# A GEGLU feed-forward kernel: TensorE transposes one block of x instead of two, and the early loads change queues

## The chip, the core and the metric

The kernel runs on one NeuronCore of a Trainium2 chip. Its engines work side by side, each through its own list of instructions, and meet at semaphores: TensorE (PE: matmuls, with weight loads as PEld), VectorE (DVE), ScalarE (ACT), GpSimd (POOL) and SyncE (SP). SP and ACT also issue DMAs, each into a queue of its own (q1 is SP's and q10 ACT's in the profile); the transfers of both run on the same 16 DMA engines. The metric is the device time of one execution in microseconds: 271.39 us, the median of four runs (271.34 to 272.06).

## The reference

x is 1024 x 1024 (32 x 32 tokens of 1024), the gate and up weights are 1024 x 3584, the down weight is 3584 x 1024, all bf16.

```python
def _gelu(x):
    return jax.nn.gelu(x, approximate=True)
...
    B, S, D, F = 32, 32, 1024, 3584
...
def reference(x, w_gate, w_up, w_down):
    return (_gelu(x @ w_gate) * (x @ w_up)) @ w_down
```

## The kernel before

**Tiling.** The 1024 of D are DK = 8 blocks of 128 (k), the 3584 of F are FM = 28 blocks of 128 (m). A matmul holds a 128 x 128 block of a weight (its stationary operand) and streams 512 tokens of x with D on the partitions, so x is needed transposed: `xT[0]` (`x0`) is the first 512 tokens as 8 blocks of 128 x 512, `xT[1]` (`x1`) the other 512. Gate and up results of four m at a time fill the eight PSUM banks, bank 2m + j with j = 0 for gate and 1 for up.

**Stages.** First come the blocks m = 0 to 9 for the first 512 tokens, in ordinary bf16 matmuls. Their weights sit in two buffers `quad[0]` (m = 0 to 3) and `quad[1]` (m = 4 to 7), each 2 (gate, up) x 8 (k) x 512 columns. Then 14 pairs of m go through a seven-product scheme on sums and differences of operands (lines 236 to 484), in fp32r, and last the product with the down weight in the same manner (487 to 616).

**The order of work.** `_Program` collects the instructions. TensorE's run in the order in which they are added; those of every other engine are sorted by a planned time `at` and, at the same `at`, by the order of adding (line 88). Each instruction waits for the last writer of what it reads and for the readers of what it overwrites; nothing else orders the engines. One DMA has one semaphore, so that one load of two k-blocks tells of both at once. All the instructions stand under line 117 in the profile, where they are emitted.

**The first 12 us.** All of this has `at` = 0, so the order in the code is the order in the queues:

- Lines 200 to 201: TensorE warms up with six matmuls of 512 columns and two of 128 on constants.
- Lines 203 to 205: NX = 2 blocks (k = 0 and 1) of x, as it lies in memory, go into `xn`, a view of the last block of `hT`. SP brings tokens 0 to 255 and ACT tokens 256 to 511, 128 KB each.
- Lines 210 to 213: `load_quad(eng, q, j, k0, k1)` loads columns of quad q, gate or up j, k-blocks k0 to k1. SP issues the four gate blocks (q = 0 and 1, k = 0 and 1), ACT the four up blocks, 128 KB each.
- Lines 214 to 215: SP issues DMA transposes of x blocks 2, 3, 4, 5 and of 6 and 7 together, from memory into `xT[0]`.
- Lines 216 to 218: ACT issues k = 2 and 3 of quad 1, gate and up in turn, and then loads its table for GELU (line 219).
- Lines 220 to 225: TensorE transposes the eight 128 x 128 pieces of `xn`, two to a PSUM bank, and VectorE copies four times two of them into `xT[0]`.
- Lines 262 to 267: quad 0 with k = 0 and 1: for each k four gate matmuls, then four up matmuls. After k = 1 the sums are copied to `kept`, by ACT for even m and by VectorE for odd m; quad 0 goes on with k = 2 to 7 much later.
- Lines 268 to 270: ACT issues k = 4 to 7 of quad 1 (`at` 9 and 10).
- Lines 273 to 287: quad 1 with all k, eight matmuls per k up to k = 5, then k = 6 and 7 one m after another. When the first matmul with k = 2 has run (`begin_late`), SP may issue k = 2 to 7 of quad 0. At `at` = 12 come the transposes of `xT[1]` (line 317).

Of the kernel before, what the change touches and what calls it, by code (L numbers as in the profile page):

```python
# [6 lines left out]
P = 128  # L7
BF16 = mybir.dt.bfloat16
# [115 lines left out]
def bass_standalone__geglu_ffn__sampling_kernel(  # L124
# [11 lines left out]
    DK, FM = D // P, F // P  # L136
# [3 lines left out]
    x_r = xf.rearrange("(tc p) d -> p tc d", p=P)  # L140
# [3 lines left out]
    pr = _Program()  # L144

    with ExitStack() as es:
        def sb(name, shape, dtype):
            return es.enter_context(nc.sbuf_tensor(name, shape, dtype))

        hT = sb("hT", [P, FM, N], BF16)  # L150
# [5 lines left out]
        ident = sb("ident", [P, P], BF16)  # L156
        warm = sb("warm", [P, 2], FP32)
        p1 = sb("p1", [P, 512], FP32)
        ps = es.enter_context(nc.psum_tensor("ps", [P, 8, 512], FP32))
        const0 = nc.const_aps.tensor(0.0, [P, 1], FP32)  # L160

        xT = [arena[:, a:a + 4096].rearrange("p (k n) -> p k n", n=512) for a in (16384, 0)]
        quad = [arena[:, a:a + 8192].rearrange("p (j k c) -> p j k c", j=2, k=DK) for a in (20480, 8192)]
        def duo(a): return arena[:, a:a + 4096].rearrange("p (j k c) -> p j k c", j=2, k=DK)
        wd = [[arena[:, a:a + 7168].rearrange("p (k n) -> p k n", n=512) for a in row] for row in ((0, 7168), (14336, 21504))]
        xn = hT[:, FM - 1, :].rearrange("p (t c) -> p t c", c=2 * P)
        Sf = S[:, :, :].bitcast(FP32)
        Tf = T[:, :, :, :, :].bitcast(FP32)
        T2r = T[:, :, :, :, :].rearrange("p u j k c -> p (u j k c)").rearrange("p (s n) -> p s n", n=512)
# [9 lines left out]
        def mm(bank, lhsT, rhs, start, stop, held=False, add=False):  # L179
            return pr.add("pe", held_matmul if held else "matmul", ps[:, bank, 0:rhs.shape[-1]], lhsT, rhs,  # L180
                          start=start, stop=stop, skip_group_check=add)
# [4 lines left out]
        def act(out, a, f, at):  # L186
            return pr.add("act", "activation", out, a, f, at=at)

        def dma(eng, out, a, at, name, after=()):
            return pr.add(eng, "dma_start", out, a, at=at, dma=name, after=after)  # L190
# [6 lines left out]
        pr.add("pool", "memset", ident[:, :], 0.0)  # L197
        pr.add("pool", "affine_select", ident[:, :], ident[:, :], [[-1, P]], ALU.not_equal, 1.0,
               base=0, channel_multiplier=1)
        for n in [512] * 6 + [P] * 2:  # L200
            mm(3, one[:, 0:P], one[:, 0:n], True, True)

        NX = 2
        for i, eng in enumerate(("sp", "act")):
            dma(eng, xn[:, 2 * i:2 * i + 2, :], x_r[:, 2 * i:2 * i + 2, 0:NX * P], 0, f"xn{i}")

        def load_quad(eng, q, j, k0, k1, at=0, after=()):
            dma(eng, quad[q][:, j, k0:k1, :], w_r[j][:, k0:k1, 4 * q * P:4 * (q + 1) * P], at, f"w{q}_{j}_{k0}", after)

        for q in range(2):  # L210
            for k in range(NX):
                load_quad("sp", q, 0, k, k + 1)
                load_quad("act", q, 1, k, k + 1)
        for k0, k1 in ((2, 3), (3, 4), (4, 5), (5, 6), (6, 8)):
            pr.add("sp", "dma_start_transpose", xT[0][:, k0:k1, :], xf[0:512, k0 * P:k1 * P], dma=f"x{k0}_0")
        for k in range(2, 4):
            for j in range(2):
                load_quad("act", 1, j, k, k + 1)
        act(warm[:, 0:1], const0, GELU, 0)
        for k in range(NX):  # L220
            for i, b in enumerate((6, 7) if k == 0 else (4, 5)):
                half = ps[:, b, 0:P].bitcast(BF16)
                for t in range(2):
                    pr.add("pe", "transpose", half[:, t * P:(t + 1) * P], xn[:, 2 * i + t, k * P:(k + 1) * P], ident[:, :])
                pr.add("dve", "tensor_copy", xT[0][:, k, i * 256:(i + 1) * 256], half)

# [3 lines left out]
        def piece(a): return a.rearrange("p t n -> p (t n)").bitcast(FP32).rearrange("p (j n) -> p j n", j=2)  # L232
        kept = [piece(hT[:, m:m + 2, :]) for m in (14, 16, 18, 20, 22, 24, 26, 10, 12)] + [piece(o11[:, :, :])]
# [10 lines left out]
        bank = lambda b: ps[:, b, :]  # L244

        def copy(eng, out, a, at):
            if eng == "act":
                act(out, a, COPY, at)
            else:
                pr.add("dve", "tensor_copy", out, a, at=at)  # L250
# [3 lines left out]
        def raw(m, j, k, b, start):  # L254
            return mm(b, quad[m // 4][:, j, k, m % 4 * P:(m % 4 + 1) * P], x0[:, k, :], start, k in (NX - 1, 3, DK - 1), add=not start and k >= NX)
# [6 lines left out]
        for k in range(NX):  # L262
            for j in range(2):
                for m in range(4):
                    raw(m, j, k, 2 * m + j, k == 0)
                    if k == NX - 1:
                        copy(("act", "dve")[m % 2], kept[m][:, j, :], bank(2 * m + j), 6.5 + 0.9 * j + 0.1 * m)
        for i, k in enumerate((4, 6)):
            for j in range(2):
                load_quad("act", 1, j, k, k + 2, 9 + i)  # L270
# [376 lines left out]
```

## Time and profile before

| what | value |
|---|---|
| median of four runs | 271.39 us |
| the profiled execution, its own time | 271.35 us |
| its span, first to last instruction | 269.8 us |
| granted TensorE clock, mean | 1.000 |
| ACT's eight weight loads, issues | 1.25 to 5.37 us |
| ACT's table load | 5.40 to 6.68 us |
| SP's x load, issue, and time from issue to landing | 0.74 us, 2.6 us |
| ACT's x load, issue, and time from issue to landing | 0.73 us, 2.8 us |
| quad 0, k = 0: gate and up, issue to landing | 2.7 and 3.0 us |
| quad 1, k = 1: gate and up, issue to landing | 4.9 and 5.1 us |
| matmul of 512 columns on real data, spacing from 4.59 us on | 0.216 us |

A row of the profile's timeline gives start and duration in us, the engine (with q: its issuing side), the line, the operation, output and inputs by name, how many, and in brackets the engine's idle time before it with what ended it. The chain of waits is followed back from the last instruction: at each step to what released it, or to the instruction before it on its engine. For matmuls the durations overlap, so that spacing counts. In a table of stretches the columns are the stretch, busy time and count for PE, PEld, DVE, ACT and POOL, the granted clock, the mean busy share of the DMA engines (it can pass 1 where packets overlap) and GB/s. A DMA row gives out<-in, the queue, the operation, how many, KB each where it is known, and us from issue to landing.

### The profile page before, as it was taken

How to read it: one execution, taken by the hardware profiler on the slowest of the kernel's cores; microseconds unless marked ns; L12 is line 12 of the kernel's file. 1: busy time of each engine (PE TensorE's matmuls, PEld its weight loads, DVE VectorE, ACT ScalarE, POOL GpSimd, SP SyncE). 2: the span in 40 equal slices, each digit the busy share in tenths (PEclk: the TensorE clock that was granted, in tenths of full speed). 3: DMA queues.
4: the chain of work that ended last, by engine and by line, in shares of the span. 5: the costliest groups of instructions: out<-in, count | busy, mean ns of one | idle time of the engine just before them, and what ended most of it. 6: DMA issues, size and time to landing. Idle time of an engine off the chain costs nothing.

```text
span 269.8 us, 3324 instructions
## 1 busy us (share of the span) xinstructions
PE 266.4 (99%) x1197; PEld 192.1 (71%) x1206; DVE 208.2 (77%) x246; ACT 136.0 (50%) x221; POOL 37.2 (14%) x23
## 2 busy tenths in 40 slices
PE   8999999999999999999999999999999999999997
PEld 3444448888888888888777676664458888888884
DVE  1348998898889889988764839289976999999921
ACT  1349876656766676667455564521220305057452
POOL 1000003203311331134345060000000000000000
PEclk9999999999999999999999999999999999999999
DMA  7999750130591002962900080293010000002102
GB/s 219 239 334 238 215 159 4 57 98 0 153 291 25 0 1 79 291 215 87 227 0 0 0 266 9 91 343 114 0 39 19 4 0 0 0 0 80 58 21 97
DMA packets 45024, 27.47 MB, mean 102 GB/s; under 512 B 8656, under 2 KB 45008, under 8 KB 45008
## 3 DMA queue, kind: packets, MB, share of 16 engines
q1 hardware_dynamic: 42496, 25.04, 33.2%
q10 hardware_dynamic: 2512, 2.23, 3.0%
q8 instruction: 9, 0.15, 0.2%
q14 instruction: 7, 0.06, 0.1%
HBM read 23.33 MB, written 2.10 MB: 94 GB/s over the span
## 4 chain that ended last, share of the span: by engine, by line
PE 99%; DVE 0%; issue 0%
PE ps L117 99%; DVE arena L117 0%; DVE o L117 0%
## 5 line engine op out<-in xcount | busy, mean ns | idle before, releaser
L117 PE MATMUL ps<-S,T 128*128 128x512 f32 x560 | 129.2, 391 | 0.0
L117 PEld LDWEIGHTS ps<-S,T 128*128 128x128 f32 x560 | 105.1, 188 | 22.4
L117 ACT ACTIVATE tmp<-ps 128x512 f32<-128x512 f32 x64 | 38.0, 596 | 51.7 <-PE ps L117 51.5
L117 POOL TENSOR_TENSOR T<-arena 128x1024 fp32r<-128x1024 bf16 x17 | 36.5, 2155 | 123.4 <-PE ps L117 81.7
L117 PE MATMUL ps<-T,S 128*128 128x512 f32 x224 | 51.3, 390 | 0.0
L117 DVE TENSOR_TENSOR T<-arena,T 128x1024 fp32r<-128x1024 bf16 x42 | 50.9, 1218 | 0.2
L117 PEld LDWEIGHTS ps<-T,S 128*128 128x128 f32 x224 | 42.0, 188 | 8.8
L117 ACT ACTIVATE ps<-ps 128x512 f32<-128x512 f32 x44 | 25.6, 583 | 37.0 <-PE ps L117 37.0
L117 DVE TENSOR_TENSOR hT<-tmp,ps 128x512 bf16<-128x512 f32 x56 | 37.0, 684 | 8.7 <-PE ps L117 6.7
L117 PE MATMUL ps<-arena 128*128 128x512 bf16 x186 | 41.6, 379 | 0.6 <-DVE arena L117 0.3
L117 DVE TENSOR_TENSOR tmp<-ps,tmp 128x512 f32<-128x512 f32 x28 | 19.4, 692 | 23.5 <-PE ps L117 23.5
L117 PEld LDWEIGHTS ps<-arena 128*128 128x128 bf16 x192 | 18.2, 98 | 23.1 <-issue 1.4
L117 DVE TENSOR_TENSOR T<-arena 128x1024 fp32r<-128x1024 bf16 x25 | 30.0, 1219 | 4.4 <-PE ps L117 4.3
L117 DVE TENSOR_TENSOR ps<-ps,tmp 128x512 f32<-128x512 f32 x32 | 22.3, 696 | 3.0 <-PE ps L117 3.0
L117 PE MATMUL ps<-arena,hT 128*128 128x512 bf16 (+2 forms) x124 | 24.3, 355 | 0.1
L117 PEld LDWEIGHTS ps<-arena,hT 128*128 128x128 bf16 x126 | 11.7, 98 | 12.7 <-issue 0.5
L117 ACT ACTIVATE tmp<-tmp 128x512 f32<-128x512 f32 x28 | 17.5, 630 | 2.4 <-DVE tmp L117 2.1
L117 ACT ACTIVATE ps<-hT 128x512 f32<-128x512 f32 x22 | 13.0, 598 | 7.6 <-DVE hT L117 7.6
L117 DVE TENSOR_TENSOR S<-hT 128x1024 fp32r<-128x1024 bf16 x14 | 16.6, 1218 | 0.0
L117 ACT ACTIVATE T<-arena 128x1024 fp32r<-128x1024 bf16 x14 | 14.8, 1059 | 0.0
L117 PE MATMUL ps<-S 128*128 128x512 f32 x56 | 12.9, 389 | 0.0
L117 ACT ACTIVATE hT<-ps 128x512 f32<-128x512 f32 x18 | 9.4, 600 | 5.9 <-PE ps L117 5.9
(33 smaller groups left out, 93.8 us busy)
## 6 DMA issues: line engine op xcount, KB each, us to landing
arena<-in_w_down_dram SPq DMA_DIRECT2D x4, 1792.0 KB, 9.6
arena<-in_w_gate_dram SPq DMA_DIRECT2D x10, 512.0 KB, 4.9
arena<-in_w_up_dram SPq DMA_DIRECT2D x10, 512.0 KB, 6.0
out_dram<-arena SPq DMA_DIRECT2D x12, 128.0 KB, 1.7
arena<-in_w_up_dram ACTq DMA_DIRECT2D x6, 128.0 KB, 5.0
arena<-in_w_gate_dram SPq DMA_DIRECT2D x3, 256.0 KB, 5.4
arena<-in_w_up_dram SPq DMA_DIRECT2D x3, 256.0 KB, 5.8
arena<-in_w_gate_dram SPq DMA_DIRECT2D x4, 128.0 KB, 4.6
```

Source lines behind the costliest of these rows:

```text
L117: ins = name(eng, *args, **kw) if callable(name) else getattr(eng, name)(*args, **kw)
```

## The change

TensorE transposes only block 0 of x. `xn` shrinks to 128 columns, so SP and ACT each load 64 KB of x. Block 1 becomes the first of SP's DMA transposes. SP issues only one weight load before them, the gate of quad 0 with k = 0; ACT issues the up of quad 0 with k = 0, then gate and up of quad 0 with k = 1, of quad 1 with k = 0 and 1 in one load of 256 KB each, and of quad 1 with k = 2 and 3 in the same way. The warm-up becomes five matmuls of 512 columns and one of 128. The copies of quad 0 to `kept` change places between ACT and VectorE. The order of the matmuls on real data stays.

```diff
-        xn = hT[:, FM - 1, :].rearrange("p (t c) -> p t c", c=2 * P)
+        xn = hT[:, FM - 1, 0:4 * P].rearrange("p (t c) -> p t c", c=P)
...
-        for n in [512] * 6 + [P] * 2:
+        for n in [512] * 5 + [P]:
             mm(3, one[:, 0:P], one[:, 0:n], True, True)
 
         NX = 2
         for i, eng in enumerate(("sp", "act")):
-            dma(eng, xn[:, 2 * i:2 * i + 2, :], x_r[:, 2 * i:2 * i + 2, 0:NX * P], 0, f"xn{i}")
+            dma(eng, xn[:, 2 * i:2 * i + 2, :], x_r[:, 2 * i:2 * i + 2, 0:P], 0, f"xn{i}")
...
-        for q in range(2):
-            for k in range(NX):
-                load_quad("sp", q, 0, k, k + 1)
-                load_quad("act", q, 1, k, k + 1)
-        for k0, k1 in ((2, 3), (3, 4), (4, 5), (5, 6), (6, 8)):
+        load_quad("sp", 0, 0, 0, 1)
+        load_quad("act", 0, 1, 0, 1)
+        for q, k0, k1 in ((0, 1, 2), (1, 0, 2), (1, 2, 4)):
+            for j in range(2):
+                load_quad("act", q, j, k0, k1)
+        for k0, k1 in ((1, 2), (2, 3), (3, 4), (4, 5), (5, 6), (6, 8)):
             pr.add("sp", "dma_start_transpose", xT[0][:, k0:k1, :], xf[0:512, k0 * P:k1 * P], dma=f"x{k0}_0")
-        for k in range(2, 4):
-            for j in range(2):
-                load_quad("act", 1, j, k, k + 1)
         act(warm[:, 0:1], const0, GELU, 0)
-        for k in range(NX):
-            for i, b in enumerate((6, 7) if k == 0 else (4, 5)):
-                half = ps[:, b, 0:P].bitcast(BF16)
-                for t in range(2):
-                    pr.add("pe", "transpose", half[:, t * P:(t + 1) * P], xn[:, 2 * i + t, k * P:(k + 1) * P], ident[:, :])
-                pr.add("dve", "tensor_copy", xT[0][:, k, i * 256:(i + 1) * 256], half)
+        for i in range(2):
+            half = ps[:, 6 + i, 0:P].bitcast(BF16)
+            for t in range(2):
+                pr.add("pe", "transpose", half[:, t * P:(t + 1) * P], xn[:, 2 * i + t, :], ident[:, :])
+            pr.add("dve", "tensor_copy", xT[0][:, 0, i * 256:(i + 1) * 256], half)
...
-                        copy(("act", "dve")[m % 2], kept[m][:, j, :], bank(2 * m + j), 6.5 + 0.9 * j + 0.1 * m)
+                        copy(("dve", "act")[m % 2], kept[m][:, j, :], bank(2 * m + j), 6.5 + 0.9 * j + 0.1 * m)
```

## The prediction

> **What bounds the kernel now.** I read the page first, for the engine shares and the chain of waits; then the chain in order of time, to see where TensorE ever stands still; then the timeline of the first 12 us with the DMA issues one by one; then stretches of that time with the DMA rate in each.
>
> ```profile
> span 269.8 us, 3324 instructions
> PE 266.4 (99%) x1197; PEld 192.1 (71%) x1206; DVE 208.2 (77%) x246; ACT 136.0 (50%) x221; POOL 37.2 (14%) x23
> ...
> PE 99%; DVE 0%; issue 0%
> ```
>
> ```profile
> 0.78 3.16 PE ps L117 x10
> 3.93 0.02 issue
> 3.96 0.50 DVE arena L117 x2
> 4.46 0.14 issue
> 4.59 7.28 PE ps L117 x33
> ...
> 191.12 76.87 PE ps L117 x355
> 268.02 0.29 DVE o L117
> ```
>
> The reader is to see that from 4.59 us to 268.02 us the end is set by TensorE alone (the "issue" pieces of 0.05 to 0.07 us in between are lost records). So the change can do two things only: move the 4.59, and open a hole behind it. Whatever lies off TensorE costs nothing until a matmul waits for it. The profiled execution took 271.35 us, 1.55 us more than its span; the median of the runs is 271.39. The sum is made against 271.35.
>
> The order of early matmuls is fixed: quad 0 with k = 0 (4 gate, 4 up), with k = 1 (8 more), then quad 1 with k = 0, 1, 2 and so on, eight per k. One takes 0.216 us (33 in 7.28, less one lost record). From 4.59 that gives the time at which each operand is first wanted now: k = 1 of quad 0 at 4.59 + 8 x 0.216 = 6.32; quad 1 gate 8.05, its up 8.91; quad 1 with k = 2 at 11.50, its up 12.37. The rows show how near the present loads come:
>
> ```profile
> 1.26 1.87 SPq L117 DMA_DIRECT2D arena<-in_w_gate_dram  x4
> 3.17 7.53 SPq L117 DMA_TRANSPOSE arena<-in_x_dram  x5
> 6.29 2.93 PEld L117 LDWEIGHTS ps<-arena 128*128 128x128 bf16 x15 [0.31 <-DMA arena<-in_w_gate_dram]
> ```
>
> The weight load at 6.29 waited for the second gate block; it landed 4.5 us after its issue at 1.75, at 6.25, just in time for 6.32. There is no slack at that point. Quad 1's blocks land at 6.95 to 7.85, some 1.0 to 2.2 us early, and x block 2 at 9.23, 2.3 us early.
>
> **The change part by part.**
>
> *Start.* The warm-up loses one matmul of 512 (0.43, the spacing of its weight loads at 2.44, 2.86, 3.29) and one of 128 (0.11): it ends at 0.78 + 5 x 0.427 + 0.107 = 3.02 instead of 3.50. Four of eight transposes and two of four copies (0.28 each) go. The transposes also wait for x, which lands now at 3.36 (SP) and 3.55 (ACT). The new loads have as many packets at half the size. No row has this load; one bound is that it lands as now, the other is that 512 packets on 16 engines each save the 9 ns between the trace's 512-byte packets (27 ns) and its 256-byte ones (18 ns), 0.29 us. From the third transpose (3.72) to the second copy (4.16) are 0.45 us, the copy takes 0.28, the matmul follows 0.15 later. With x there at 3.07 and 3.26 the first matmul starts at about 4.15, with x as now at 4.45. I take 4.25, a gain of 0.34 us. The copies removed were hidden behind matmuls.
>
> *x block 1.* SP has x at 0.74, gate k = 0 at 1.26, and then the transpose at 1.75 instead of three more gates. The other five transposes follow at 1.25 to 1.31 us each (2.3 for the last): 3.0, 4.3, 5.6, 6.9, 8.2, each about 0.17 earlier than now. Two rows bound the landing:
>
> ```profile
> arena<-in_x_dram SPq DMA_TRANSPOSE x1, 6.1
> ```
>
> ```profile
> arena<-in_x_dram SPq DMA_TRANSPOSE x1, 3.5
> ```
>
> The first is the present first transpose (issue 3.17), the second one of two blocks at 21.62 with no weight loads beside it. So block 1 lands between 5.25 and 7.85; wanted at 4.25 + 1.73 = 5.98. The 6.1 contains a wait behind four gates in SP's queue, of which only one is left in front now: the first transpose landed 1.6 us after the last of these gates (7.61). First gate at 3.7 + 1.6 = 5.3; with the 2.1 that lay between the first two transposes, 5.8. I take 5.6: in time, with little to spare.
>
> *Quad 0, k = 1.* Gate and up are now ACT's third and fourth issue (1.80, 2.28); the nearest rows landed at 6.45 and 7.14, with one packet in the lot held 1.4 us. Less x stands before them now. I take 5.2 and 5.8 against wants of 5.98 and 6.84.
>
> *Quad 1.* All of its early weights go to ACT's queue as four loads of two k-blocks, the gate of k = 0 and 1 at 2.76. ACT has eight issues instead of nine, at 0.45 to 0.68 each, so its table load (1.28) starts at about 5.0 instead of 5.40 and it is free for copies at 6.5; the first bank is due at 6.35 and now goes to VectorE, which is idle then. The swap of copies costs nothing; with that cover gone bank 0 is still free by 7.1, wanted at 7.7. What does matter: a load of two blocks tells of its landing once, so the block of k = 1, wanted at 9.77 and 10.63 before, has to be there at 8.05 and 8.91 with that of k = 0. And SP, which carried half of these weights, now carries only transposes from 3 us on. Until now they began to move after 6.1. The stretches show what they do to the rate (the last two numbers are the DMA share and GB/s):
>
> ```profile
> 5.25:6.25 1.00, 1.00 (x6) 0.38 (x4) 0.00 (x0) 0.85 (x1) 0.00 (x0) 1.00 1.08 366
> 6.25:7.25 1.00, 1.00 (x7) 0.49 (x6) 0.30 (x1) 0.99 (x3) 0.00 (x0) 1.00 1.97 251
> 7.25:7.75 0.50, 0.50 (x4) 0.23 (x3) 0.50 (x2) 0.50 (x2) 0.00 (x0) 1.00 0.16 32
> 7.75:8.50 0.75, 0.75 (x6) 0.32 (x4) 0.75 (x2) 0.75 (x3) 0.00 (x0) 1.00 0.93 296
> 8.50:9.50 1.00, 1.00 (x6) 0.38 (x5) 0.93 (x2) 0.35 (x1) 0.00 (x0) 1.00 1.33 244
> 9.50:10.50 1.00, 1.00 (x7) 0.53 (x6) 0.00 (x0) 0.00 (x0) 0.00 (x0) 1.00 1.54 165
> 10.50:11.25 0.75, 0.75 (x5) 0.31 (x4) 0.00 (x0) 0.00 (x0) 0.00 (x0) 1.00 1.04 212
> ```
>
> Weights alone move at 366 GB/s; from 6.25 to 11.25, with transposes among them, the mean is 211, and at 7.25 to 7.75 both queues stand. By the time the up load of quad 1 (k = 0, 1) has landed, the new order has moved x (131 kB), quad 0's and quad 1's blocks (1049 kB) and three transposes (393 kB): 1573 kB. By 3.25 us some 310 kB of it are through (352 now, 131 fewer of x, 88 more in the 0.29 us saved). 1263 kB at 211 take 5.99 us: 9.24, and 0.4 from last packet to landing, as for the first x load: 9.64. At 366 it would be 7.1, at 165 it would be 11.3. By a third way, the bytes alone, the present kernel had landed as much at about 9.2. I take 211, since transposes now run through the whole stretch.
>
> *Sum.* The up matmuls of quad 1 start at 9.64 instead of 8.91: +0.73, in which the early start is already used up. Behind that the later wants move too, by the same 0.73; the up load of k = 2, 3 has to move some 786 kB more (524 and two transposes) at 211, so it lands at 13.4 against 12.37 + 0.73 = 13.1: 0.3 more at worst, in the range. 271.35 + 0.73 = 272.1.
>
> The Trainium skill, Advanced Engine Details and Errata, section X-Bar Transpose (TRN2), says that transposing transfers are as fast as ordinary ones. The stretches above speak against it: 366 without, 211 with them. By the rule the up load would land at 7.1 and the time would be 271.0.
>
> **Rivals.** *All in time* (not slower): transposes give way to ACT's 1024-byte packets, or fewer than three are through by 9 us. Then only the start counts, 4.25 for 4.59: 271.0, at best 270.9. For it: at 7.75 to 8.50 nearly all that moved was ACT's, at 296. Against it: the two stretches after. It decides if the up load lands before 8.57.
>
> *A draw by bytes*: the queues reach the 9.2 of the present order: +0.3, 271.65.
>
> *x block 1 is late*: its landing is the 7.85 of the present first transpose, and TensorE stands from 5.98 on: 7.85 - 6.32 = +1.5, 272.9. For it: a packet of a weight block was held 1.4 us at 3.87, and the first transpose's packets stood until 7.85, about when SP's last gate landed. A transpose that waits for the slowest DMA engine has no slack in the new order. It decides from a landing after 6.32.
>
> *The clock stays low*: the warm-up matmuls run 0.43 us apart, those from 4.59 on 0.216, so the clock rose in between. With 0.5 us less warm-up and a gap before the first matmul it may rise one such period later: the 3.2 us from 0.78 to about 4.0 once more, to 7.2. (7.2 - 4.25)/2 = 1.5 lost, 0.34 gained: +1.1, 272.5. Against it: the gap grows by some 0.3 us only.
>
> The Trainium skill, TensorE: Matmul & The Clock Gate, section Part 4: PE-mode transpose, says that transposes do not count as work for the clock. The trace can't show that alone; if so, the busy part before 4.0 falls from 2.7 to 2.2 us, which favours this rival.
>
> **How the numbers follow.** Forecast (late weights, 271.9 to 272.6) 0.36; late x 0.12; low clock 0.10; a draw 0.20; all in time 0.22. Slower by over 0.2% (0.54 us, about what a measurement of this kernel can tell from no change) are the first three: 0.58. Within it: the draw and most of the last, 0.36. Faster: what is left of the last, 0.06, since even the best start gives 0.48. The likeliest time is 272.1. The range goes from 271.0 to 273.0: below, all in time; above, late x or the 165 GB/s in part. The forecast's own range is 271.9 to 272.6.
>
> **What would show it.** Start right: the first matmul of 512 on real data at 4.15 to 4.45, four transposes. Late weights: a weight-load wait on w_up (ACT's queue) of 0.5 to 1.2 us near 8.5, transposes moving from 3.3 on, rates near 211 GB/s. Late x: the wait stands at 6 and names in_x. Low clock: matmuls 0.43 apart after 4.25. It is wrong if TensorE has no hole before 13 us, or a hole after it.

## The result, and the profile after

| | before | changed |
|---|---|---|
| median | 271.66 us (74 runs) | 272.21 us (53 runs) |
| lowest, highest | 271.31, 272.48 | 271.51, 273.9 |
| ratio of the times | | 1.0018, 95% interval 1.0011 to 1.0024 |
| the profiled execution, its span | 271.35, 269.8 | 271.91, 270.6 |

The changed kernel is slower by 0.55 us, and with so many runs that is clear of chance. It lies on the 0.2% bound of the prediction: the ratio of 1.0018 is just inside, the difference of the medians, 0.55 for 0.54 us, just outside. With 74 runs the median of before stands 0.27 us above the 271.39 of its first four.

The page of the changed kernel's profile, its span and engine shares:

```profile
span 270.6 us, 3304 instructions
PE 267.0 (99%) x1191; PEld 191.9 (71%) x1200; DVE 207.7 (77%) x244; ACT 136.2 (50%) x221; POOL 37.2 (14%) x23
```

The chain of waits in order of time (start, us, what), changed kernel:

```profile
0.78 2.63 PE ps L117 x8
3.40 0.02 issue
3.42 0.52 DVE arena L117 x2
3.94 0.14 issue
4.08 9.87 PE ps L117 x39
...
191.93 76.87 PE ps L117 x355
268.80 0.02 issue
268.82 0.29 DVE o L117
```

The first real matmul starts at 4.08 instead of 4.59, so 0.51 us are won there; and yet the last piece starts 0.8 us later. From 4.08 us on there is no hole on the chain: TensorE stands still for no load. The loss shows only in the spacing of the matmuls. The timeline of weight loads, changed kernel:

```profile
4.05 0.14 PEld L117 LDWEIGHTS ps<-arena 128*128 128x128 bf16 x2 [0.71 <-DMA arena<-in_w_gate_dram]
4.46 0.15 PEld L117 LDWEIGHTS ps<-arena 128*128 128x128 bf16 x1 [0.28 <-issue]
4.88 0.15 PEld L117 LDWEIGHTS ps<-arena 128*128 128x128 bf16 x1 [0.28 <-issue]
5.31 0.15 PEld L117 LDWEIGHTS ps<-arena 128*128 128x128 bf16 x1 [0.28 <-issue]
5.74 0.15 PEld L117 LDWEIGHTS ps<-arena 128*128 128x128 bf16 x1 [0.28 <-issue]
6.17 0.15 PEld L117 LDWEIGHTS ps<-arena 128*128 128x128 bf16 x1 [0.28 <-issue]
6.59 2.76 PEld L117 LDWEIGHTS ps<-arena 128*128 128x128 bf16 x13 [0.28 <-issue]
9.52 0.26 PEld L117 LDWEIGHTS ps<-arena 128*128 128x128 bf16 x2 [0.17 <-DMA arena<-in_w_up_dram]
```

The weight loads are 0.43 us apart until 6.59, as in the warm-up, and then 0.22: the matmuls ran at half speed to about 6.7. The first up matmul of quad 1, the 21st on real data, started at 9.68; at 0.216 a matmul it would have been 4.08 + 20 x 0.216 = 8.40. So the low clock cost 1.28 us in this execution; less the 0.51 won at the start that is 0.77, nearly the whole difference of the spans (0.8). The last row shows the other thing. Quad 1's up load landed at 9.48, just before it was wanted at this slow pace. Had the clock been up and the load no earlier, it would have been wanted at 8.4 and TensorE would have stood for about a microsecond. Two costs lie over each other here, and one profile can't say which of them sets the median.

The stretches (the last number is GB/s) show the loads, changed kernel:

```profile
4.25:5.25 1.00, 1.00 (x3) 0.29 (x2) 0.00 (x0) 0.18 (x1) 0.00 (x0) 1.00 1.08 190
5.25:6.25 1.00, 1.00 (x4) 0.38 (x3) 0.00 (x0) 1.00 (x1) 0.00 (x0) 1.00 1.03 256
6.25:7.25 1.00, 1.00 (x5) 0.41 (x4) 0.00 (x0) 0.31 (x2) 0.00 (x0) 1.00 1.21 184
7.25:8.25 1.00, 1.00 (x7) 0.47 (x5) 0.74 (x2) 0.53 (x2) 0.00 (x0) 1.00 1.19 250
```

Between 4 and 8 us the rate is 184 to 256 GB/s; before the change it was 291 and 366 in the first two of these stretches. The column of the granted clock reads 1.00 even where the matmuls run at half speed (this trace holds no record of it), so the clock has to be read from the spacing.

### The profile page after: what moved, and what is told of

It reads as the page before. It is cut to its first block, busy times and chain, and to the rows that moved or that the text cites. A ratio compares the mean times of both kernels' runs of the same rounds, so it can differ in the third digit from the quotient of the medians.

```text
span 270.6 us, 3304 instructions
## 1 busy us (share of the span) xinstructions
PE 267.0 (99%) x1191; PEld 191.9 (71%) x1200; DVE 207.7 (77%) x244; ACT 136.2 (50%) x221; POOL 37.2 (14%) x23
## 4 chain that ended last, share of the span: by engine, by line
PE 99%; DVE 0%; issue 0%
PE ps L117 99%; DVE arena L117 0%; DVE o L117 0%
## 5 line engine op out<-in xcount | busy, mean ns | idle before, releaser
L117 PE MATMUL ps<-arena 128*128 128x512 bf16 x186 | 42.9, 387 | 0.8 <-DVE arena L117 0.5
```

Source lines behind the costliest of these rows:

```text
L117: ins = name(eng, *args, **kw) if callable(name) else getattr(eng, name)(*args, **kw)
```

## The experiments

All ran beside the kernel before on the same chip; each difference is against the before of its own group (medians 271.78, 271.59 and 271.76 us). "Up" is the landing of quad 1's first up load in the profiled execution, "x1" that of x block 1 by its transpose, "first" the first real matmul, "clock" the time at which the spacing of the matmuls falls from 0.43 to 0.22 us.

| kernel | median, lowest, highest | against before | ratio, 95% | first | x1 | up | clock |
|---|---|---|---|---|---|---|---|
| short warm-up alone | 272.11, 271.07, 273.38 | +0.33 | 1.0000 to 1.0030 | 4.32 | - | 6.25 | 4.1 |
| queues alone | 272.61, 271.40, 273.53 | +0.83 | 1.0002 to 1.0039 | 4.49 | - | 10.18 | 3.7 |
| transposes held | 271.45, 271.08, 272.67 | -0.33 | 0.9973 to 0.9998 | 4.30 | 5.92 | 8.35 | 8.0 |
| single blocks | 272.34, 271.79, 273.36 | +0.56 | 1.0009 to 1.0037 | 4.08 | 6.58 | 8.25 | 6.4 |
| gap filled | 271.85, 271.50, 274.14 | +0.26 | 0.9993 to 1.0030 | 4.07 | 6.54 | 10.20 | 4.2 |
| held and filled | 271.52, 271.24, 272.24 | -0.07 | 0.9980 to 1.0004 | 4.12 | 6.56 | 8.42 | 4.2 |
| long warm-up | 272.25, 271.55, 273.90 | +0.66 | 1.0003 to 1.0035 | 4.81 | 6.43 | 10.07 | 10.0 |
| gate on SP | 272.90, 271.89, 273.27 | +1.31 | 1.0024 to 1.0052 | 4.10 | 6.17 | 7.91 | before 4.1 |
| block 1 first | 271.46, 271.01, 271.99 | -0.30 | 0.9977 to 0.9997 | 4.07 | 5.41 | 8.63 | 4.5 |
| block 1 first, gap open | 271.69, 270.89, 274.11 | -0.07 | 0.9994 to 1.0038 | 4.07 | 5.86 | 8.38 | 5.4 |
| warm-up of four | 273.53, 273.17, 273.70 | +1.77 | 1.0049 to 1.0076 | 4.76 | - | 6.59 | 8.1 |
| held, again | 271.43, 270.86, 272.01 | -0.33 | 0.9979 to 0.9999 | 4.07 | 6.03 | 8.21 | 4.9 |

Twelve runs each, ten of "gate on SP" and five of "warm-up of four". For the kernels with the old load order and for the single blocks "up" is the block of k = 0 alone.

**Short warm-up alone**, on the kernel before:

```diff
-        for n in [512] * 6 + [P] * 2:
+        for n in [512] * 5 + [P]:
```

> The kernel before with only the shorter warm-up (five matmuls of 512 columns and one of 128). Late weights: nothing of the loads has changed, so within 0.1 us of before, and the fastest runs as before (about 271.3). Low clock: the shorter warm-up by itself lets the clock rise later in more runs, median 0.3 to 0.6 us above before, with runs above 272.5.

Measured +0.33, with an interval from 1.0000. The lowest run is 0.27 below the lowest of before, as its start is (4.32 for 4.59); but 4 of 12 runs are above 272.5, where none of the 74 runs of before is. No load was touched. So the shorter warm-up wins its start in some runs and loses more in others, which speaks for the low clock and against "within 0.1". It is not shown in a trace: the profiled execution is the fastest of the twelve, with the clock up at 4.1.

**Queues alone**, the kernel before with only the order of the weight loads changed:

```diff
-        for q in range(2):
-            for k in range(NX):
-                load_quad("sp", q, 0, k, k + 1)
-                load_quad("act", q, 1, k, k + 1)
+        load_quad("sp", 0, 0, 0, 1)
+        load_quad("act", 0, 1, 0, 1)
+        for q, k0, k1 in ((0, 1, 2), (1, 0, 2), (1, 2, 4)):
+            for j in range(2):
+                load_quad("act", q, j, k0, k1)
...
-        for k in range(2, 4):
-            for j in range(2):
-                load_quad("act", 1, j, k, k + 1)
```

> The kernel before with only the new order of the weight loads: SP issues one gate block and then its five transposes, ACT all other early weights, quad 1 in loads of two k-blocks; TensorE still transposes two blocks of x behind the full warm-up. Late weights: quad 1's up load lands at 9.2 to 9.8 us, wanted at 8.9; the fastest runs rise by 0.3 or more to about 271.7, the median by 0.4 to 0.8. Low clock: within 0.1 us of before, since TensorE's work up to the first real matmul is as before.

Here the clock was up by 3.7 us in the profiled execution, so that the loads show alone. Its rows of weight loads on TensorE:

```profile
7.42 0.55 PEld L117 LDWEIGHTS ps<-arena 128*128 128x128 bf16 x4 [0.67 <-DMA arena<-in_w_up_dram]
8.39 0.55 PEld L117 LDWEIGHTS ps<-arena 128*128 128x128 bf16 x4 [0.43 <-DMA arena<-in_w_gate_dram]
10.22 2.70 PEld L117 LDWEIGHTS ps<-arena 128*128 128x128 bf16 x14 [1.29 <-DMA arena<-in_w_up_dram]
```

Each of the three rows begins with a wait for a load of ACT's queue: the up of quad 0 with k = 1 (landed at 7.37), then gate and up of quad 1 (8.35 and 10.18, later than expected). TensorE's holes there are 0.34, 0.10 and 0.96 us (distance of the two matmuls less 0.216), 1.4 in all, and the span is 271.1, 1.3 above before. The median rose by 0.83. That is late weights, without a change in TensorE's work. The lowest run, 271.40, rose by only 0.06 and not by the 0.3 expected: the lateness differs from run to run.

**Transposes held**, the changed kernel with SP's transposes of blocks 2 to 7 waiting for the fifth real matmul; run in two groups:

```diff
+        pr.add("sp", "dma_start_transpose", xT[0][:, 1:2, :], xf[0:512, P:2 * P], dma="x1_0")
-        for k0, k1 in ((1, 2), (2, 3), (3, 4), (4, 5), (5, 6), (6, 8)):
...
+                    done = raw(m, j, k, 2 * m + j, k == 0)
+                    if (k, j, m) == (0, 1, 0):
+                        hold = done
...
+        for k0, k1 in ((2, 3), (3, 4), (4, 5), (5, 6), (6, 8)):
+            pr.add("sp", "dma_start_transpose", xT[0][:, k0:k1, :], xf[0:512, k0 * P:k1 * P], dma=f"x{k0}_0",
+                   after=[hold] if k0 == 2 else ())
```

> The changed kernel, in which SP holds the transposes of x blocks 2 to 7 until the fifth matmul on real data has run (at about 5 us instead of 3.0). Late weights: quad 1's up load lands near 8.3 instead of 9.5, and the fastest runs fall to 270.9 to 271.2, the median by 0.3 to 0.6 below the changed kernel. Low clock: as the changed kernel, +0.4 to +0.7 against before, fastest run about 271.5.

> The held kernel once more, beside the three above. If its lead was more than chance of the clock: median again 0.2 to 0.4 below before, fastest run near 271.1; if it was chance, within 0.1 of before.

The median is both times 0.33 below before, while the changed kernel is 0.55 above it: the hold gives back some 0.9 us, more than expected, and makes a version faster than both. The up load landed at 8.35 and 8.21 instead of 9.48. Nothing but SP's transposes was moved, so they are what made it late. The DMA rate shows how. From 6.25 to 8.25 us the changed kernel moved 184 and 250 GB/s, with transposes among the weights; the held kernel (second group), whose transposes move only from 8.1 us on, has:

```profile
6.25:7.25 1.00, 1.00 (x6) 0.45 (x5) 0.62 (x2) 0.49 (x2) 0.00 (x0) 1.00 1.06 354
7.25:8.25 1.00, 1.00 (x6) 0.48 (x5) 1.00 (x3) 1.00 (x3) 0.00 (x0) 1.00 1.10 362
```

The weight loads of the same run:

```profile
4.46 0.15 PEld L117 LDWEIGHTS ps<-arena 128*128 128x128 bf16 x1 [0.28 <-issue]
4.88 0.99 PEld L117 LDWEIGHTS ps<-arena 128*128 128x128 bf16 x5 [0.28 <-issue]
6.13 2.33 PEld L117 LDWEIGHTS ps<-arena 128*128 128x128 bf16 x12 [0.26 <-issue]
8.63 0.27 PEld L117 LDWEIGHTS ps<-arena 128*128 128x128 bf16 x2 [0.16 <-issue]
```

From 4.46 on no row names a DMA, and the lowest run (270.86) is 0.48 below the lowest of before in its group: nearly all of the 0.52 us won at the start. The low clock was still there: in the profile of the first group it rose at 8.0, and that execution took 272.67.

**Single blocks**, the changed kernel with quad 1's first loads split:

```diff
-        for q, k0, k1 in ((0, 1, 2), (1, 0, 2), (1, 2, 4)):
+        for q, k0, k1 in ((0, 1, 2), (1, 0, 1), (1, 1, 2), (1, 2, 4)):
```

> The changed kernel with quad 1's loads of k = 0 and 1 as four loads of one block (gate 0, up 0, gate 1, up 1). Late weights: the up block of k = 0 is 262 kB less deep in the queue order and lands some 0.6 to 1.2 us earlier than 9.5; the fastest runs fall by 0.2 to 0.5 below the changed kernel's 271.5. Low clock: no difference from the changed kernel beyond 0.1 us.

The up block landed 1.2 us earlier, as expected, and the time did not fall: +0.56, as in the changed kernel. The next load is late in its place: the up of k = 2 and 3 landed at 13.06, where it was 12.33 in the changed kernel; at full pace it is wanted at 4.08 + 36 x 0.216 = 11.86, and TensorE had a hole of 0.15 there although the clock was low to 6.4. The expectation looked at one want and not at the queue behind it.

**Gate on SP**, the changed kernel with quad 1's first gate load between SP's first two transposes, and no longer on ACT's queue:

```diff
...
+        pr.add("sp", "dma_start_transpose", xT[0][:, 1:2, :], xf[0:512, P:2 * P], dma="x1_0")
+        load_quad("sp", 1, 0, 0, 2)
```

> The changed kernel, but SP issues quad 1's gate load of k = 0 and 1 between its first and its second transpose, so that ACT's queue has 262 kB less ahead of the up load. Late weights: the up load lands 0.7 to 1.2 us earlier than 9.5 and the other transposes begin later; fastest run 271.0 to 271.3, median 0.3 to 0.6 below the changed kernel. Low clock: as the changed kernel (+0.4 to +0.7 against before).

Wrong. The up load came 1.6 us earlier (7.91), but the gate 1.8 us later (9.48 for 7.63), and TensorE waited 1.5 us for it. The gate was issued at 3.01, and its packets moved only from 5.4 to 8.5 us, when those of block 1, ahead of it in SP's queue, were through (5.0). Of two loads wanted one after the other, the slower one sets the time.

**Gap filled, held and filled, long warm-up.** In the first two, five matmuls of 128 on constants stand between the transposes and the first real matmul; the second has the hold too; the third is the changed kernel with the warm-up of before.

```diff
+        for n in [P] * 5:
+            mm(3, one[:, 0:P], one[:, 0:n], True, True)
```

> The changed kernel with five more matmuls of 128 columns on constants between TensorE's transposes and the first real matmul, where it stands idle for 0.5 us. Low clock: the clock rises in time in more runs; runs above 272.7 go, the median falls by 0.2 to 0.5 below the changed kernel. Late weights: the floor stays at the changed kernel's 271.5, since the loads are as before, and the median does not fall below 271.7.

> Both: the transposes of x blocks 2 to 7 held until the fifth real matmul, and the five small matmuls in the gap. If late weights and low clock are two separate costs, both go: fastest run 271.0 to 271.2, median 271.2 to 271.5, no run above 272.4, and it beats both kernels. If the clock alone explained the changed kernel, this would be no better than the filling alone.

> The changed kernel with the warm-up of before (six of 512, two of 128), to 3.5 us. The first real matmul starts at about 4.5 instead of 4.08. Low clock: fewer runs above 272.5, the median 0.1 to 0.4 below the changed kernel. Late weights: the floor stays at 271.5, since a start 0.4 later is hidden in the wait for quad 1's up load at 9.5.

The filled kernel's clock was up at 4.2, and so it shows the changed kernel's loads without the clock (in an execution of 272.47 us, 0.6 above its median, so that the holes of most runs are smaller):

```profile
6.64 0.56 PEld L117 LDWEIGHTS ps<-arena 128*128 128x128 bf16 x4 [1.10 <-issue]
7.50 0.56 PEld L117 LDWEIGHTS ps<-arena 128*128 128x128 bf16 x4 [0.30 <-DMA arena<-in_w_up_dram]
8.52 0.54 PEld L117 LDWEIGHTS ps<-arena 128*128 128x128 bf16 x4 [0.46 <-DMA arena<-in_w_gate_dram]
10.25 2.71 PEld L117 LDWEIGHTS ps<-arena 128*128 128x128 bf16 x14 [1.19 <-DMA arena<-in_w_up_dram]
```

The holes between the matmuls are 0.79 at 5.9 (x block 1, landed at 6.54), 0.13 (quad 1's gate) and 0.85 (its up): 1.8 us, and the span is 271.2. Its median, +0.26, can't be told from the changed kernel's +0.55 or from before, and two runs are at 273.4 and 274.1; that the filling helps by itself is not shown. With the hold the up load's hole is gone, the one of 0.82 for block 1 stays, and the time is that of before; it was expected to beat both kernels. The long warm-up was expected to be better than the short and is not (+0.66). In its profile the first gate landed at 4.77, TensorE stood from 3.92 to 4.81, and the clock rose only at 10.0.

**Block 1 first**, without and with the gap open: the transpose of block 1 is SP's first issue behind x, and ACT carries the first gate; with the hold.

```diff
-        load_quad("sp", 0, 0, 0, 1)
+        load_quad("act", 0, 0, 0, 1)
```

> Held transposes and filled gap, and in addition the transpose of x block 1 as SP's first issue after x, with the first gate load on ACT. In the filled and held kernel block 1 landed at 6.56 and TensorE stood 0.8 us for it. Late x: the issue at 1.26 instead of 1.75 brings the landing to 5.9 to 6.1, the hole falls to 0.1 to 0.3, fastest run 270.9 to 271.1, median 0.3 below the held and filled kernel's 271.52. If the landing is set by traffic and not by its issue, it stays at 6.4 or later and the time at 271.5.

> The same without the small matmuls in the gap. Low clock: a gap of 0.7 us or more before the first real matmul, so a share of runs above 272.2, median 0.1 to 0.4 above the filled one. If the clock does not see the gap, equal to the filled one within 0.1.

Issued 0.5 us earlier and with no gate load ahead of it, block 1 landed at 5.41, 1.15 earlier than in the held and filled kernel and earlier than expected, and its hole was gone: what is left are holes of 0.09 on quad 0's first up load and of 0.09 on quad 1's gate. The time is -0.30 against before, equal to the held kernel. With the gap open the median is 0.23 higher, as expected for the low clock, but the interval reaches from below before to above it; 5 of 12 runs are above 272.5; the clock may be the cause, but the two runs of the held kernel have an open gap as well, and there it is 1 of 24. In this kernel the first up load also landed late (5.63, wanted at 4.94 at full pace). It stays open which of the two makes these runs.

**Warm-up of four**, on the kernel before:

```diff
-        for n in [512] * 6 + [P] * 2:
+        for n in [512] * 4:
```

> The kernel before with a warm-up of four matmuls of 512 alone, to 2.5 us, so that TensorE stands for about 0.7 us until x lands; all loads as before. Low clock: more runs in which the clock rises one period later; median 0.5 to 1.2 above before, runs up to 273.5, the fastest as before or 0.3 below. Late weights: no change beyond 0.1 in the median.

+1.77 with an interval clear of 1, more than expected, and no load was changed. Its weight loads:

```profile
3.66 0.78 PEld L117 LDWEIGHTS ps<-ident,hT 128*128 128x128 bf16 x8 [1.93 <-DMA hT<-in_x_dram]
...
7.28 0.15 PEld L117 LDWEIGHTS ps<-arena 128*128 128x128 bf16 x1 [0.28 <-issue]
7.70 0.15 PEld L117 LDWEIGHTS ps<-arena 128*128 128x128 bf16 x1 [0.28 <-issue]
8.11 0.96 PEld L117 LDWEIGHTS ps<-arena 128*128 128x128 bf16 x5 [0.26 <-issue]
```

TensorE was without work for 1.2 us before the transposes (from 2.44, the end of the fourth matmul, to 3.66), and the first real matmuls ran at half speed, to 8.1: 8.1 - 4.76 is 3.3, half of it 1.7 us, and the start was 0.17 later; the span is 1.8 longer. So too little work ahead of the first real matmul does cost clock, with all weights in time.

## Why the prediction was right or wrong

**The size.** Forecast 272.1, measured 272.21; that they lie so near is in part luck. The sum started from 271.35, 0.31 below the median of before in 74 runs, and its rise of 0.73 was 0.18 above the 0.55 measured.

**The signs.** By the prediction's own signs the profiled execution is the low clock: matmuls 0.43 apart after 4.25, and no hole before 13 us, which it had named as a sign of being wrong. Late weights decide in other executions, and that is known from the experiments.

**The start** was mis-sized: 0.34 forecast, 0.51 measured. The loads of x landed at 2.92 and 3.08, earlier than the better of the two bounds (3.07 and 3.26), so the first matmul came at 4.08, outside 4.15 to 4.45.

**Late weights**, the mechanism of the forecast, is shown, but not by the changed kernel's own profile: by the holes where the clock was up (queues alone, gap filled) and by the hold, which takes the lateness away and 0.9 us with it. The landing of 9.64 was 9.48 in the changed kernel, 10.18 and 10.20 in the two where the clock was up. It was right for reasons that cancel: from 3.25 to 9.08 us the changed kernel moved 234 GB/s and not 211, but also 1364 kB and not 1263. By 9.08 only 292 kB of transposes were through for 393, but 1260 kB of weights for 1049, since ACT's next load already moved beside the one that was waited for.

**The next want** was put at 13.4 for the up of k = 2 and 3; it landed at 12.33 in the changed kernel, at 13.06 where the load before it was split, at 13.28 with the queues alone. It decides nothing until the first lateness is mended halfway, as the single blocks show. A reading of the present loads was off as well: quad 1's blocks (6.95 to 7.85) land 1.1 to 2.8 us before their wants and not 1.0 to 2.2.

**x block 1 in time** is the step that failed. It was put 1.6 us after the landing of the load ahead of it, as the trace of before had it; the changed kernel shows 6.20 - 3.85 = 2.35. Wanted at 5.81 with the clock up and a start at 4.08, the block landed at 5.92 to 6.58 in every profile in which its transpose has SP's first gate load ahead of it, and cost 0.5 to 0.8 us of TensorE in the three where the clock didn't hide it (gate on SP, gap filled, held and filled). Its bytes were not late: its 512 packets had moved by 5.10 in the changed kernel, 1.1 us before it landed, and by 4.80 in the filled one, 1.7 before. The prediction's way from last packet to landing, 0.4 us, was taken from the first x load. What the transpose waits for there is not shown. The rival of a late x was given as 1.5 us at a landing of 7.85; TensorE does stand for block 1, at half the price. Quad 0 with k = 1, also taken to be in time, was so in the changed kernel (4.78 and 6.11), and its up cost 0.34 us with the queues alone.

**The low clock** was given one chance in ten and was what the profiled execution shows, 1.28 lost and 0.51 won where 1.5 and 0.34 had been put. Warm-up runs on the kernel before show that less work ahead of the first matmul costs by itself (+0.33, with an interval from 1.0000, and +1.77). The forecast took the cases as exclusive. They are not: a low clock and a late load hide each other, because a want that comes later is no longer late. The medians allow one sum: the start won 0.51, the hold takes 0.88 off the changed kernel, so of the +0.55 the transposes beside the weights make 0.88, and 0.18 is left for the clock and what the hold doesn't mend. In another order of mending the shares would differ, but the transposes are the larger part.

## What to carry to other kernels

When a load moves to another queue, ask what now moves beside it: here SP's transposes, which nobody wanted for more than 8 us, took the DMA engines from weights that were wanted at once, and a wait of one instruction in front of them was worth 0.9 us. Where TensorE starts cold, a start won by a shorter warm-up can be lost again to the clock, and a hole hidden by a slow clock is still there. And a single profile may show only one of the two, so read several executions before naming a cause.

## What the runs showed of the hardware

- The clock does not rise at a fixed time after the first matmul: the profiles have it between 3.7 and 10.0 us, always with the first warm-up matmul at 0.78. Seven traces hold a record of the granted clock, which agrees with the spacing (3.96 us before the change, 10.00 in the long warm-up). Full speed lasts 266.24 us in six of them and 262.83 in the seventh: 3.41 less, and 266.24 is 78 times 3.413. So the clock changes as if in steps of 3.41 us that lie differently in each execution. Go back in such steps from the rise, in thirteen of the fourteen profiles (with the gate on SP the rise falls into a pause): in the step that ends with the rise TensorE has work for 2.73 us or more, in those before it, where the clock stays low, for at most 2.55 (changed; 2.52 long warm-up, 2.50 held, 1.99 warm-up of four). A pause of 0.68 us within a step is let pass, one of 0.89 costs a step more. The Trainium skill, TensorE: Matmul & The Clock Gate, section Part 1: The HAM clock gate (the "warmup" mystery), has a window of about 3.4 us that runs free of the kernel and must be busy. The traces agree with such a window, and with a bound between 2.55 and 2.73 us of work in it.
- TensorE's transposes count as such work here. Without them the step that ends with the rise has only 2.19 us in the short warm-up, while 2.40 us of warm-up matmuls alone, in the first step of the long warm-up, did not raise the clock. The page that the prediction quotes on this is not borne out, and the rival of the low clock gains nothing from it.
- Weights alone moved at 354 and 362 GB/s in the held kernel (6.25 to 8.25 us) and at 366 before the change (5.25 to 6.25), but at 268 and 291 in the stretches of 1 us ahead of these; weights with DMA transposes of 128 KB among them at 184 and 250 in the changed kernel (6.25 to 8.25).
- Behind a transpose in the same queue a load of 256 KB needed 6.5 us from issue to landing (gate on SP, 3.01 to 9.48); on the other queue, issued 0.25 us before, one of the same size needed 5.2 (2.76 to 7.91). The work ahead of the two differs, so this is not the price of the transpose alone.
